# Attention and a feed-forward block on one core: where the second weight matrix, batch 2's transposes and the reserve of feed-forward work stand in the program

## The chip, the cores and the metric

The kernel runs on one core of a Trainium2 chip. A core has a matrix engine (TensorE, PE in the profile), a vector engine (VectorE, DVE), an activation engine (ScalarE, ACT), a general engine (GpSimd, POOL), a queue engine (SyncE, SP) and 16 DMA engines. Each engine runs its own list of instructions in order; they wait for each other by semaphores. The metric is the time of one execution in microseconds of device time, the median of three runs.

## The reference, cut to what matters

```python
# 8 batches, 8 heads, 576 positions, head size 64; 512 model columns, 2048 hidden columns
scores = scale * np.matmul(q, k.transpose(0, 1, 3, 2))
cum    = np.cumsum(np.maximum(s, 0.0), axis=-1)
bias   = -(cum[:, :, :, None] - cum[:, :, None, :])
scores = np.where(causal, -1e9, scores + np.minimum(bias, 0.0))
attn   = softmax(scores)
x      = np.matmul(attn, v)  # then (batch, position, 8 heads * 64)
xn     = (x - mean) / np.sqrt(var + 1e-06) * g_ln
out    = x + np.maximum(xn @ w_ch1, 0.0) @ w_ch2
```

Attention has a bias that sinks with the running sum of a gate, and a causal mask. Its output goes through a layer norm and two matrix products with a ReLU between them.

## The kernel before

**Tiles.** 576 positions are four full tiles of 128 and a tail of 64. q and k of all heads of a batch stand in `aug` as bf16, with four extra columns that carry the running sum (`shift` writes these). Transposed, they stand in `qkT`: 68 rows, 16 heads of q and k. The tails of two batches are put together (`xts`), and those of four batches make one small chunk of the feed-forward block (`tail_chunk`).

**Groups.** The main loop at the end (lines 621 to 642) runs over `g`, one group for each head of each batch: group 8b+h is head h of batch b. A group issues the scores of its head (`score_mms`, line 163), the exponentials on ACT and the mask on POOL (`score_exp`), the products with v of the group before (`values`, line 209), and a number of feed-forward units between them. The values of a batch's last head come at the end of its last group, in `last_of` (line 598).

**Units.** The feed-forward block of a batch (its chunk) is cut into 32 units of four matmuls of 128x512: 16 for the first product and 16 for the second (a tail chunk has 16 units). `chunk_units` appends them to the list `units`; `mlp(n)` takes n from its head and issues them. A chunk can only be appended when its norm has been issued, which is at the end of its batch. So a queue of units of the batch before fills PE beside the attention of the present one. `n_units` (line 620) sets how many each group takes: 2 or 3 in groups 8 to 15, then 4,4,4,4,3,3,3,3 for each batch.

**The end of a batch.** `last_of(b)` issues the last values, then for two halves: statistics and `norm` (DVE writes `xn`, POOL raises the variance to the power -1/2), a DMA transpose of `xn` on SP (`x_t`), and two units.

**How q, k and v come in.** Batches 0 to 2 are loaded head by head into buffers of their own (`homes`), 128 KB a request, all asked for by SP: 24 requests for heads and 3 for tails. Some of these buffers are used again: batch 2's q lies where batch 1's k was, its k where batch 1's v was, its v where batch 1's q was. DVE and POOL cast q and k of a head into `aug` (`cast_head`), PE transposes them (`t_pe`, `t_act`, ten transposes a head), and DVE and ACT copy the two results to `qkT`. From batch 3 on the loads go by tiles through `ring`, ten slots; POOL casts, SP issues DMA transposes (`t_dma`, one for each of the five tiles), and each cast gives a slot back (`room`), which lets `loads()` ask for the next tile.

**What sets the order.** `at(g, pos, f)` hangs a function into group g, at one of the places "a", "a2", "b", "x", "c", "d", "e" in it. On each engine instructions run in the order in which the program issues them; a load waits on SP until its buffer's last reader is through.

Of the kernel before, what the change touches and what calls it, by code (L numbers as in the profile page):

```python
# [16 lines left out]
def kernel(  # L17
# [11 lines left out]
    nc = tc.nc  # L29

    B, H, S, D = q.shape
# [20 lines left out]
    AHEAD = 10  # L52
# [56 lines left out]
    def copy(eng, o, i):  # L109
        if eng == "act":  # L110
            nc.scalar.copy(out=o, in_=i)  # L111
        elif eng == "dve":
            nc.vector.tensor_copy(out=o, in_=i)  # L113
        else:
            nc.gpsimd.tensor_copy(out=o, in_=i)  # L115
# [12 lines left out]
    def shift(b, eng):  # L128
        hb = slice(b * H, (b + 1) * H)
        eng.tensor_scalar_mul(out=aug[:, :, 0:H, D], in0=cumh[:, :, hb, 0], scalar1=-1.0)  # L130
        eng.tensor_copy(out=aug[:, :, H:HD, D1:DK], in_=cumh[:, :, hb, :])
# [6 lines left out]
    def load_w2(i):  # L138
        nc.gpsimd.dma_start(out=w2_bf[:, 4 * i : 4 * i + 4, :], in_=w2_r[:, 4 * i : 4 * i + 4, :])
# [4 lines left out]
    def new_t(b):  # L144
        qkT[b] = tpool.tile([P, HD, SP_], BF16, name="qkT", tag="qkT")

    def t_pe(b, h, engs=("dve", "dve")):
        for j, eng in ((h, engs[0]), (H + h, engs[1])):
            pt = ps_m.tile([P, 2 * 512], BF16, name="pt", tag="pm")
            for p in range(NT):  # L150
                nc.tensor.transpose(pt[0:DK, p * P : (p + 1) * P], aug[:, p, j, 0:DK], ident)  # L151
            copy(eng, qkT[b][0:DK, j, :], pt[0:DK, 0:SP_])

    def t_dma(b, p):
        nc.sync.dma_start_transpose(
            out=qkT[b][:, :, p * P : (p + 1) * P],
            in_=aug[:, p, :, :].rearrange("p h d -> p (h d)"),
        )
# [50 lines left out]
    def values(g):  # L209
        b, h = g // H, g % H  # L210
        pot = pots.pop(g)[0]
        e = ebufs[g % 3]
        for t in range(NT):
            for kb in range(t + 1):
                c = EO[kb] + (t - kb) * P
                if t == NF and b % 2:
                    c -= TL
                nc.tensor.matmul(  # L218
                    pot[:, t * D1 : (t + 1) * D1], lhsT=e[:, c : c + P],
                    rhs=v_bfs[b % 2][:, kb, h, :], start=(kb == 0), stop=(kb == t),  # L220
                )
        xs[b] = xbufs[(2, 1, 0)[b % 3]]
        pv = pot[:, 0 : NT * D1].rearrange("p (t d) -> p t d", d=D1)
        rinv = small.tile([P, NT], F32, name="rinv", tag="rinv")
        rv = rinv.rearrange("p (t o) -> p t o", o=1)
        nc.vector.reciprocal(out=rv, in_=pv[:, :, D:D1])  # L226
        nc.vector.tensor_tensor(  # L227
            out=xs[b][:, :, h * D : (h + 1) * D], in0=pv[:, :, 0:D],
            in1=rv.to_broadcast([P, NT, D]), op=ALU.mult,
        )  # L230
        if h == H - 1:
            lo = TL * (b % 2)
            nc.gpsimd.tensor_copy(
                out=xts[b // 2 % 3][lo : lo + TL, :], in_=xs[b][lo : lo + TL, NF, :]
            )


    units = []
# [15 lines left out]
    def stores(eng, keep=0):  # L254
        while len(late) > keep:
            o, i = late.pop(0)
            eng.dma_start(out=o, in_=i)
# [98 lines left out]
    def mlp(n, eng=None):  # L356
        for _ in range(min(n, len(units))):
            stores(eng or nc.scalar, 0 if eng else 1)
            units.pop(0)()
# [14 lines left out]
    def tails_in(what, b, eng):  # L374
        t = homes[what, b]
        eng.dma_start(
            out=t[0:TL, :, NF, :],
            in_=src[what][b, :, NF * P : S, :].rearrange("h s d -> s h d"),
        )

    def head_in(what, b, h, eng):
        t = homes[what, b]
        eng.dma_start(  # L383
            out=t[:, h, 0:NF, :],
            in_=src[what][b, h, 0 : NF * P, :].rearrange("(t p) d -> p t d", p=P),
        )

    def cast_head(what, b, h, eng):
        i = homes[what, b][:, h, :, :]
        o = v_bfs[b % 2][:, :, h, 0:D] if what == "v" else aug[:, :, (what == "k") * H + h, 0:D]  # L390
        copy(eng, o, i)
# [9 lines left out]
    n_loaded, room = [0], [0]  # L401

    def loads():
        while n_loaded[0] < len(seq) and room[0] > 0:
            key = seq[n_loaded[0]]
            t = ring[:, n_loaded[0] % AHEAD, :]
            room[0] -= 1
            dma_in(t, src_of(src[key[0]], key[1], key[2]), nc.sync)
            staged[key] = t
            n_loaded[0] += 1  # L410

    def casts(what, b, p, eng):
        cast((what, b, p), eng)
        room[0] += 1
# [64 lines left out]
    NG = B * H  # L479
    hooks = {}  # L480

    def at(g, pos, f):
        hooks.setdefault((g, pos), []).append(f)

    def run(g, pos):
        for f in hooks.get((g, pos), ()):
            f()
# [21 lines left out]
    def heads_in(b, hs):  # L509
        for h in hs:  # L510
            for what in "qkv":
                head_in(what, b, h, nc.sync)
# [12 lines left out]
    def tiles(c, i, part, lo, hi):  # L525
        for a in i:
            stats(c, a, part, lo, hi)

    def t_act(b, h):
        t_pe(b, h, ("dve", "act"))  # L530

    def c_head(b, h):
        cast_head("q", b, h, "dve")
        cast_head("k", b, h, "pool")
# [23 lines left out]
    for h in range(H):  # L558
        at(8 + h, "a", lambda h=h: feed(1, h))
        if h >= 2:  # L560
            at(7 + h // 2, "a2" if h % 2 else "c", lambda h=h: t_act(1, h))
    for i in range(4):
        at(9 + i, "e", lambda i=i: load_w2(i))
    for p in (3, 4):
        at(6 + p, "e", lambda p=p: nc.gpsimd.memset(aug[:, p, :, DK:P], 0.0))


    for g, hs in ((9, (0, 1)), (10, (2, 3)), (11, (4, 5))):
        at(g, "b", lambda hs=hs: heads_in(2, hs))

    def b2_rest():
        for what in "qkv":
            tails_in(what, 2, nc.sync)
        heads_in(2, (6, 7))

    at(12, "a", b2_rest)
    at(13, "e", lambda: (new_t(2), shift(2, nc.gpsimd)))
    for h in range(H):
        g = 12 + h // 2
        at(g, "d", lambda h=h: c_head(2, h))  # L580
        at(g + 2, "a2" if h % 2 else "c", lambda h=h: t_act(2, h))
        at(g + 1, "d", lambda h=h: cast_head("v", 2, h, "pool"))

    def more(n):
        room[0] += n

    at(16, "e", lambda: more(AHEAD))


    for b in range(3, B):  # L590
        g0 = 8 * (b - 1) + (2 if b == 3 else 0)
        at(g0, "a", lambda b=b: (shift(b, nc.gpsimd), new_t(b)))
        for p in range(NT):
            at(g0 + p, "d", lambda b=b, p=p: (casts("q", b, p, "pool"), casts("k", b, p, "pool")))
            at(g0 + p + 1, "c", lambda b=b, p=p: t_dma(b, p))
            at(min(g0 + 5 + p // 2, 8 * b - 1), "d", lambda b=b, p=p: casts("v", b, p, "pool"))

    def last_of(b):
        values(8 * b + 7)
        for i in ((0, 1), (2, 3)):  # L600
            tiles(b, i, 1, 256, 512)
            norm(b, i, 2)
            x_t(b, i)
            mlp(2)
        chunk_units(b)

    def tail_chunk(c):
        tiles(c, (0, 1), 0, 0, 512)
        norm(c, (0, 1), 1)
        x_t(c, (0, 1))  # L610
        chunk_units(c)

    for b in range(B):
        at(8 * b + 5, "d", lambda b=b: tiles(b, range(NF), 0, 0, 256))
        if b:
            at(8 * b + 7, "e", lambda b=b: last_of(b))
        if b % 4 == 3:
            at(8 * b + 8, "x", lambda b=b: tail_chunk(B + b // 4))

    n_units = {g: 2 + (g in (9, 11, 13, 14, 15)) if g < 16 else 4 - (g % H > 3) for g in range(H, NG)}  # L620
    for g in range(NG + 4):
        nu = n_units.get(g, 0 if g < H else 4)
        run(g, "a")
        if g >= 3:
            loads()
        if g < NG:
            score_mms(g)
            run(g, "a2")
            score_exp(g, 0)
        mlp(min(1, nu))  # L630
        if g < NG:
            score_exp(g, 1)
        mlp(min(1, nu - 1))
        run(g, "b")
        if 1 <= g <= NG and g % H:
            values(g - 1)
        run(g, "x")
        run(g, "c")
        mlp(min(1, nu - 2))
        run(g, "d")  # L640
        mlp(min(1, nu - 3))
        run(g, "e")
# [32 lines left out]
```

## Time and profile before

| | |
|---|---|
| runs | 394.97, 395.89, 399.01 us |
| the profiled execution | 400.01 us |
| its span, first to last instruction | 398.3 us |
| mean granted clock of TensorE | 0.959 |
| busy in the span | PE 354.4, DVE 201.0, POOL 169.3, ACT 159.4 us |
| moved by DMA | 60.16 MB, mean 151 GB/s |

The page of the profile has a strip of 40 slices of about 10 us for each engine, in which a digit is the busy share in tenths. An answer by windows gives for each stretch its length, then for PE, PEld (weight loads), DVE, ACT and POOL the busy time and the count of instructions, then the granted TensorE clock, the DMA share and GB/s. A timeline row has start, duration, engine, source line, operation, what it writes and reads, its shape and count, and in brackets how long the engine sat idle before it and what ended that wait. Matmuls of PE are pipelined, so a row's duration overlaps the next row's start. Rows of SPq are requests on the DMA queue.

### The profile page before, as it was taken

The page shows a single profiled execution, that of the slowest core. Times are in us where ns is not written, and L with a number is a line of the kernel's source. Part 1 is how long each engine was busy: PE and PEld are TensorE (multiplying, and loading weights), DVE is VectorE, ACT ScalarE, POOL GpSimd, SP SyncE. Part 2 cuts the span into 40 slices and gives each one's busy share as a digit, 9 for nine tenths or more (in the row PEclk, how much of TensorE's full clock was granted, in tenths as well). Part 3 has the DMA queues.
Part 4 walks back from the last instruction along what each step waited for, and adds up shares of the span by engine and source line. Part 5 has one row for each costly group of instructions (what it writes and reads, how often), then busy time and mean ns, then how long its engine had stood idle before and what let it go on. Part 6 is the DMA issues. An engine that isn't in the chain of part 4 may idle for free.

```text
span 398.3 us, 7510 instructions
## 1 busy us (share of the span) xinstructions
PE 354.4 (89%) x2795; PEld 197.4 (50%) x2821; DVE 201.0 (50%) x465; ACT 159.4 (40%) x286; POOL 169.3 (43%) x331
## 2 busy tenths in 40 slices
PE   2865899399999499999997999999999998999995
PEld 1643565265555145554553575545545554444472
DVE  6588453447544614567456234743583259333231
ACT  1463486052664035615641345543553352022020
POOL 5595364446345534357455434554561124100000
PEclk9995799889999879999999899999999999999999
DMA  9999999804999999997999999979612103310112
GB/s 166 220 169 193 225 186 224 155 14 116 225 193 219 178 214 232 205 219 186 186 199 186 203 224 241 195 161 235 133 28 53 55 26 62 98 53 2 70 38 54
DMA packets 191717, 60.16 MB, mean 151 GB/s; under 512 B 182784, under 2 KB 186880, under 8 KB 191680
## 3 DMA queue, kind: packets, MB, share of 16 engines
q1 hardware_dynamic: 181952, 48.00, 65.6%
q0 software_dynamic: 4224, 4.19, 6.8%
q10 hardware_dynamic: 5504, 7.47, 6.3%
q8 instruction: 22, 0.36, 0.4%
q14 instruction: 15, 0.12, 0.1%
HBM read 37.11 MB, written 9.44 MB: 117 GB/s over the span
## 4 chain that ended last, share of the span: by engine, by line
PE 70%; DMA 11%; DVE 7%; SPq 4%; POOL 3%; issue 2%; ACT 2%; ACTq 0%; DVEq 0%; POOLq 0%
PE ph L327 27%; PE py L338 26%; PE s L171 8%; PE pot L218 6%; DMA qkT<-aug 4%; SPq L383 3%; PE pt L151 3%; DVE xn L277 3%; DMA ring<-in_q_dram 2%; DMA ring<-in_k_dram 2%; DVE stats L262 1%; POOL v_bf L115 1%; ACT e L188 1%; DVE hT L312 1%; DMA ring<-in_v_dram 1%
## 5 line engine op out<-in xcount | busy, mean ns | idle before, releaser
L338 PE MATMUL py<-w_bf,hT 128*128 128x512 bf16 x550 | 136.0, 390 | 1.4
L188 ACT ACTIVATE e<-s 128x1024 bf16<-128x1024 f32 (+1 forms) x128 | 97.8, 807 | 93.6 <-PE s L171 73.1
L327 PE MATMUL ph<-xnT,w_bf 128*128 128x512 bf16 x512 | 122.9, 383 | 3.6 <-DVE hT L312 1.9
L191 POOL TENSOR_SCALAR_AFFINE_SELECT e<-e 128x384 bf16<-128x384 bf16 (+1 forms) x128 | 56.5, 465 | 125.4 <-ACT e L188 113.4
L327 PEld LDWEIGHTS <-w_bf 128*128 128x128 bf16 x640 | 59.0, 98 | 54.7 <-issue 6.9
L338 PEld LDWEIGHTS <-hT 128*128 128x128 bf16 x576 | 54.1, 100 | 58.6 <-issue 6.1
L310 ACT ACTIVATE hT<-ph 128x512 bf16<-128x512 f32 x72 | 43.0, 597 | 91.0 <-PE ph L327 88.9
L312 DVE TENSOR_SCALAR hT<-ph 128x512 bf16<-128x512 f32 x72 | 49.4, 690 | 55.6 <-PE ph L327 54.5
L171 PE MATMUL s<-qkT 68*128 68x512 bf16 (+4 forms) x320 | 54.5, 300 | 9.9 <-DMA qkT<-aug 9.1
L171 PEld LDWEIGHTS <-qkT 68*128 68x128 bf16 x384 | 32.9, 99 | 49.4 <-issue 11.4
L344 DVE SCALAR_TENSOR_TENSOR yo<-py,rstd,x 128x512 f32<-128x512 f32 x32 | 24.0, 749 | 60.1 <-PE py L338 57.3
L115 POOL CAST aug<-ring 128x512 bf16<-128x512 f32 (+2 forms) x74 | 39.7, 559 | 17.1 <-DMA ring<-in_k_dram 17.0
L218 PEld LDWEIGHTS <-e 128*128 128x128 bf16 x960 | 38.5, 99 | 13.6 <-issue 0.5
L218 PE MATMUL pot<-v_bf,e 128*128 128x65 bf16 x960 | 40.8, 196 | 0.4 <-POOL e L191 0.4
L226 DVE RECIPROCAL rinv<-pot 128x5 f32<-128x5 f32 x64 | 12.3, 192 | 41.2 <-PE pot L218 37.9
L227 DVE TENSOR_TENSOR x<-pot,rinv 128x320 f32<-128x320 f32 x64 | 31.5, 492 | 2.5 <-DVE rinv L226 0.2
L151 PE MATMUL pt<-ident,aug 128*68 128x128 bf16 x240 | 21.1, 243 | 6.8 <-POOL aug L130 3.1
L111 ACT COPY qkT<-pt 68x640 bf16<-68x640 bf16 x17 | 11.7, 687 | 32.5 <-PE pt L151 27.0
L262 DVE BATCH_NORM_STATS2 stats<-x 128x6 f32<-128x256 f32 (+2 forms) x68 | 23.4, 398 | 0.3
L277 DVE SCALAR_TENSOR_TENSOR xn<-x,mv,gln_b 128x512 bf16<-128x512 f32 x32 | 22.6, 747 | 0.0
L151 PEld LDWEIGHTS <-aug 128*68 128x68 bf16 x240 | 17.8, 130 | 9.3 <-issue 3.2
L113 DVE COPY qkT<-pt 68x640 bf16<-68x640 bf16 x31 | 14.5, 481 | 12.2 <-PE pt L151 12.1
(55 smaller groups left out, 163.9 us busy)
## 6 DMA issues: line engine op xcount, KB each, us to landing
out_dram<-yo ACTq DMA_DIRECT2D x25, 256.0 KB, 3.3
ring<-in_q_dram SPq DMA_DIRECT2D x20, 256.0 KB, 4.3
ring<-in_k_dram SPq DMA_DIRECT2D x20, 256.0 KB, 4.9
ring<-in_v_dram SPq DMA_DIRECT2D x20, 256.0 KB, 4.5
w_bf<-in_moe_w_ch_dram POOLq DMA_DIRECT2D x8, 512.0 KB, 8.6
ring<-in_k_dram SPq DMA_DIRECT2D x31, 128.0 KB, 4.0
ring<-in_q_dram SPq DMA_DIRECT2D x22, 128.0 KB, 4.4
x<-in_v_dram SPq DMA_DIRECT2D x17, 128.0 KB, 4.0
```

Source lines behind the costliest of these rows:

```text
L115: nc.gpsimd.tensor_copy(out=o, in_=i)
L151: nc.tensor.transpose(pt[0:DK, p * P : (p + 1) * P], aug[:, p, j, 0:DK], ident)
L171: nc.tensor.matmul(o, lhsT=qkT[b][0:DK, H + h, kb * P : (kb + 1) * P], rhs=qkT[b][0:DK, h, lo:hi], start=True, stop=True,)
L188: nc.scalar.activation(out=o, in_=i, func=ACT.Exp, scale=scale)
L191: nc.gpsimd.affine_select(out=d, in_=d, compare_op=ALU.is_ge, fill=0.0, base=0, pattern=[[0, d.shape[1]], [1, P]], channel_multiplier=-1,)
L218: nc.tensor.matmul(pot[:, t * D1 : (t + 1) * D1], lhsT=e[:, c : c + P], rhs=v_bfs[b % 2][:, kb, h, :], start=(kb == 0), stop=(kb == t),)
L227: nc.vector.tensor_tensor(out=xs[b][:, :, h * D : (h + 1) * D], in0=pv[:, :, 0:D], in1=rv.to_broadcast([P, NT, D]), op=ALU.mult,)
L277: eng.scalar_tensor_tensor(out=xn[:, j, :], in0=x_of(c, a), scalar=mv[:, j, 0:1], in1=gln_b, op0=ALU.subtract, op1=ALU.mult,)
L310: nc.scalar.activation(out=o, in_=i, func=ACT.Relu)
L312: nc.vector.tensor_scalar_max(out=o, in0=i, scalar1=0.0)
L327: nc.tensor.matmul(ph[:, j * tok : (j + 1) * tok], lhsT=w1_bf[:, kd, fb * P : (fb + 1) * P], rhs=xnT[c][:, :, kd, :], start=(kd == 0), sto ...
L338: nc.tensor.matmul(st["py"], lhsT=st["h"][:, fb, a * P : (a + 1) * P], rhs=w2_bf[:, fb, :], start=(fb == 0), stop=(fb == FB - 1),)
```

## The change

Five things are done.

1. The four loads of the second weight matrix (`load_w2`, on POOL's queue) move from the ends of groups 9 to 12 to the places "b" of groups 8, 8, 9 and 10.
2. Batch 2's loads move from groups 9, 10, 11 and 12 to groups 12, 13 and 14, and its tails go first.
3. Batch 2's casts and transposes, which were spread over groups 12 to 17, go into `second_chunk` at the end of group 15: after `last_of(1)` comes `shift` (on DVE instead of POOL), then for each head one unit, the next head's cast and this head's transposes. The casts of v follow there and in groups 16 and 17.
4. The ten ring slots for batch 3 are released there too, in group 15 instead of 16, and batch 3's casts and DMA transposes begin in group 17 instead of 18.
5. Groups 8 to 15 take two units each. From group 16 on a group takes as many (at most four) as leave ten units queued at the end of its batch.

```diff
-    for i in range(4):
-        at(9 + i, "e", lambda i=i: load_w2(i))
+    for i, g in enumerate((8, 8, 9, 10)):
+        at(g, "b", lambda i=i: load_w2(i))
...
-    for g, hs in ((9, (0, 1)), (10, (2, 3)), (11, (4, 5))):
-        at(g, "b", lambda hs=hs: heads_in(2, hs))
-
-    def b2_rest():
-        for what in "qkv":
-            tails_in(what, 2, nc.sync)
-        heads_in(2, (6, 7))
-
-    at(12, "a", b2_rest)
-    at(13, "e", lambda: (new_t(2), shift(2, nc.gpsimd)))
-    for h in range(H):
-        g = 12 + h // 2
-        at(g, "d", lambda h=h: c_head(2, h))
-        at(g + 2, "a2" if h % 2 else "c", lambda h=h: t_act(2, h))
-        at(g + 1, "d", lambda h=h: cast_head("v", 2, h, "pool"))
-
-    def more(n):
-        room[0] += n
-
-    at(16, "e", lambda: more(AHEAD))
+    def b2_in(g):
+        if g == 12:
+            for what in "qkv":
+                tails_in(what, 2, nc.sync)
+        heads_in(2, range(3 * (g - 12), min(H, 3 * (g - 12) + 3)))
+
+    for g in (12, 13, 14):
+        at(g, "a", lambda g=g: b2_in(g))
+
+    def second_chunk():
+        last_of(1)
+        new_t(2)
+        shift(2, nc.vector)
+        c_head(2, 0)
+        for h in range(H):
+            mlp(1)
+            if h + 1 < H:
+                c_head(2, h + 1)
+            t_act(2, h)
+        for h in range(4):
+            cast_head("v", 2, h, "pool")
+        room[0] += AHEAD
+
+    at(15, "e", second_chunk)
+    for h in range(4, H):
+        at(14 + h // 2, "b", lambda h=h: cast_head("v", 2, h, "pool"))
...
-        g0 = 8 * (b - 1) + (2 if b == 3 else 0)
+        g0 = 8 * (b - 1) + (1 if b == 3 else 0)
...
-        if b:
+        if b > 1:
             at(8 * b + 7, "e", lambda b=b: last_of(b))
...
-    n_units = {g: 2 + (g in (9, 11, 13, 14, 15)) if g < 16 else 4 - (g % H > 3) for g in range(H, NG)}
+    n_units = {g: 2 for g in range(H, 2 * H)}
+    KEEP = 10
     for g in range(NG + 4):
+
         nu = n_units.get(g, 0 if g < H else 4)
+        if 2 * H <= g < NG:
+            nu = max(0, -((KEEP - len(units)) // (H - g % H)))
```

## The prediction

> **What bounds the kernel.** I read the page's slices first, then windows of 10 us, then PE's timeline at the slices where PE sags, then the queues for which PE waited there.
>
> ```profile
> PE   2865899399999499999997999999999998999995
> ...
> 70.00:80.00 10.00, 3.34 (x21) 1.91 (x20) 4.66 (x12) 1.08 (x2) 4.66 (x11) 0.79 0.85 147
> 80.00:90.00 10.00, 9.89 (x104) 6.25 (x105) 5.06 (x14) 4.70 (x9) 4.68 (x12) 0.87 0.07 27
> ...
> 130.00:140.00 10.00, 3.61 (x18) 1.45 (x17) 5.86 (x14) 0.00 (x0) 5.21 (x9) 0.86 1.20 183
> 140.00:150.00 10.00, 9.95 (x56) 4.64 (x57) 2.43 (x5) 3.85 (x7) 4.50 (x10) 0.80 1.18 216
> ...
> 210.00:220.00 10.00, 7.20 (x60) 3.77 (x60) 6.56 (x17) 1.08 (x3) 6.12 (x10) 0.95 1.23 181
> 220.00:230.00 10.00, 9.95 (x73) 6.09 (x73) 2.88 (x5) 3.90 (x9) 4.00 (x8) 0.87 1.31 208
> ```
>
> PE is the bound: 9 in nearly every slice. After the start-up three places sag, at 70, 130 and 210 us. In the windows PE's busy time follows the length; the granted clock and the DMA share come near the end, and the clock is short behind each sag.
>
> ```profile
> 69.92 0.82 PE L171 MATMUL s<-qkT 68*128 68x512 bf16 x5
> 74.32 0.20 PE L171 MATMUL pot<-qkT 68*128 68x64 bf16 x1 [3.58 <-DVE x L227]
> 77.60 1.28 PE L151 MATMUL pt<-ident,aug 128*68 128x128 bf16 x10 [3.08 <-POOL aug L130]
> ...
> 136.50 0.38 PE L171 MATMUL s<-qkT 68*128 68x512 bf16 x1 [3.35 <-DMA qkT<-aug]
> 139.91 1.01 PE L171 MATMUL s<-qkT 68*128 68x64 bf16 x4 [3.04 <-DMA qkT<-aug]
> ...
> 215.57 0.38 PE L171 MATMUL s<-qkT 68*128 68x512 bf16 x1
> 218.71 0.67 PE L171 MATMUL s<-qkT 68*128 68x64 bf16 x4 [2.75 <-DMA qkT<-aug]
> ...
> 72.15 0.88 DVE L113 CAST aug<-ring 128x320 bf16<-128x320 f32 x2 [5.38 <-DMA ring<-in_q_dram]
> ```
>
> Stall A (group 14): batch 2's q comes late, DVE stands 5.38 us in front of its cast, and PE idles 3.58+3.08=6.7 us. Stalls B (group 24) and C (group 40) are waits for the last DMA transposes of batches 3 and 5, 3.35+3.04=6.4 and 2.75 us. The clock missing from the windows (0.21+0.13, 0.14+0.20, 0.05+0.13, times 10 us) makes half-clock stretches of 6.8, 6.8 and 3.6 us; PE worked in about 5, 4 and 3.4 us of them and lost half: 2.5, 2.0 and 1.7 us. So A costs 9.2, B 8.4, C 4.4 us. These 22 us are about all there is to win.
>
> **The change, part by part.** Prices, from undisturbed groups and from batch 1's norm as it runs now:
>
> ```profile
> 121.61 0.82 PE L171 MATMUL s<-qkT 68*128 68x512 bf16 x5
> ...
> 124.02 0.62 PE L218 MATMUL pot<-v_bf,e 128*128 128x65 bf16 x15
> 124.47 1.03 PE L338 MATMUL py<-w_bf,hT 128*128 128x512 bf16 x4
> 125.34 0.82 PE L171 MATMUL s<-qkT 68*128 68x512 bf16 x5
> ...
> 55.74 0.73 PE L151 MATMUL pt<-ident,aug 128*68 128x128 bf16 x10
> 56.30 1.89 PE L327 MATMUL ph<-xnT,w_bf 128*128 128x512 bf16 x8
> ...
> 66.83 0.20 PE L171 MATMUL pot<-qkT 68*128 68x64 bf16 x1 [0.37 <-DVE x L227]
> ...
> 89.04 0.63 PE L218 MATMUL pot<-v_bf,e 128*128 128x65 bf16 x15
> 92.95 0.82 PE L171 MATMUL s<-qkT 68*128 68x512 bf16 x5
> ...
> 94.32 1.40 DVE L277 SCALAR_TENSOR_TENSOR xn<-x,mv,gln_b 128x512 bf16<-128x512 f32 x2
> ...
> 95.22 1.07 POOL L283 TENSOR_TENSOR rstd<-rstd,nhalf 128x2 f32<-128x2 f32 x1
> ...
> L111 ACT COPY qkT<-pt 68x640 bf16<-68x640 bf16 x17 | 11.7, 687 | 32.5 <-PE pt L151 27.0
> L113 DVE COPY qkT<-pt 68x640 bf16<-68x640 bf16 x31 | 14.5, 481 | 12.2 <-PE pt L151 12.1
> ```
>
> From start to start a unit takes 0.87 us, values 0.45, a head's ten transposes 0.56, and a group of three units 3.73, which leaves 0.68 for scores.
>
> *Two units a group in groups 8 to 15* (16 for 21). Group 14's scores move from 69.92 by three units less, 2.6, and by 0.37 more: with two units nothing stands between a group's values and the next scores, which the row at 66.83 shows as a wait, and group 12 now has it too. So 67.7; groups 14 and 15 last 0.68+1.73+0.45+0.37=3.2 up to their values, and values(15) starts at 74.6, with 0.5 us (an estimate) for the mask that it now follows directly.
>
> *Batch 2's transposes behind batch 1's norm.* values(15) at 89.04, last xn done at 95.72, 6.7 us later on DVE, POOL's rstd done at 96.29: this chain stays. Behind it now queue shift (0.4, an estimate: about one cast) and the first casts (0.44, half of the 0.88 at 72.15), so the first transpose is ready some 7.7 us after values(15). PE has values and five units meanwhile, 4.8 us: a **new stall of 2.9 us**. Then come eight heads of 0.56 and seven units, 10.5 us; each head's copies (0.48 on DVE, 0.69 on ACT) and next cast hide behind the unit of 0.87. Uncovered, an ACT copy would cost 0.69 a head, 5.5 us. Group 16 starts at 74.6+7.7+10.5=92.8, against 92.95: no sooner, but with 34 units queued for 37 (2.6 us) and four heads' transposes already done (2.25 us). Of these 5.0 us I take off 0.85, half of C's clock loss, since the clock may or may not fall behind the new stall: **A is worth 4.2 us**.
>
> The Trainium skill, "TensorE: Matmul & The Clock Gate", "What's actually happening", has the clock halved after at least one idle window of about 3.4 us. C differs: 2.75 us of idle time was enough in this trace. By the page's rule the new stall costs no clock and A is worth 5.0; by the row at 218.71 it costs C's whole 1.7 and A is worth 3.3.
>
> *Loads reordered.*
>
> ```profile
> 25.80 2.92 SPq L383 DMA_DIRECT2D ring<-in_v_dram  x1
> ...
> 47.68 0.46 SPq L383 DMA_DIRECT2D ring<-in_q_dram  x1
> ...
> 59.62 2.78 SPq L383 DMA_DIRECT2D ring<-in_k_dram  x1
> ...
> 73.25 0.50 SPq L383 DMA_DIRECT2D x<-in_v_dram  x1
> ...
> 61.09 0.48 POOL L115 CAST v_bf<-ring 128x320 bf16<-128x320 f32 x1
> ```
>
> SP asks for batch 2 from 47.68 already, whatever group the code names: only its order and free buffers count. Now the tails come first, and k's overwrites all of batch 1's v, whose last cast is at 61.09. So the 27 requests start near 61, and the down weights have the DMA alone before. SP's eleven requests from 59.62 to 73.75 took 1.28 us each beside weights; alone one takes 0.5 (73.25). At a mean of 0.9 the last goes out at 85 and lands some 4 us later; head 7 is wanted at 74.6+7.7+7x1.43=92 (1.43 is 0.56+0.87). Cost 0, covered by the norm with 3 us to spare; the third rival prices it uncovered. xnT(1)'s transposes queue on SP behind these 27, but the first unit that reads them comes ten units after last_of(1). The weights are wanted from group 15 on, five groups after the last of their requests; POOL's four issues only change places.
>
> *Batch 3 a group sooner, its loads released at 15 instead of 16.*
>
> ```profile
> 104.96 0.82 PE L171 MATMUL s<-qkT 68*128 68x512 bf16 x5
> ...
> 110.33 4.00 SPq L155 DMA_TRANSPOSE qkT<-aug  x1
> ...
> 132.61 7.26 DMA qkT<-aug
> ...
> 187.33 4.19 SPq L155 DMA_TRANSPOSE qkT<-aug  x1
> ...
> 208.13 10.53 DMA qkT<-aug
> ...
> 178.44 0.82 PE L171 MATMUL s<-qkT 68*128 68x512 bf16 x5
> ...
> DMA to landing us min/median/max: 5.1/6.4/7.0
> ```
>
> The last row is for the five transposes from 145 to 185 us, batch 4's. Batch 3's ten loads wait for batch 2's casts to free their slots, and land before group 17. There the first cast on POOL stands behind the mask and two casts of v that moved (0.9): group 17 starts at 92.8+0.85+3.3=97, and the transpose follows its group's scores by some 6.3 us, 5.4 as in batch 3 now (104.96 to 110.33) and the 0.9: 103.2. From there SP paces, a transpose of about 4 us and two loads at a time: 22.3 us from first to fifth in batch 3, 20.8 in batch 5. Landing took 7.3 and 10.5; the five of batch 4 took 5.1 to 7.0 us. So 103.2+20.8+5=129 to 103.2+22.3+10.5=136; I take 131, nearest to 22.3 and 5 to 7, since fewer of batch 3's own loads are in flight by then. PE is ready at 93.6+8x3.73+3.5=127 (eight groups, last_of(2)'s four units). The stall is 4 us and C's clock loss 1.7: **B is worth 8.4-5.7=2.7 us**. x of values(16) must now wait for the moved v casts; some 0.3 us, left out.
>
> *Ten units kept.* Groups 16 to 23 run three units where they had 4,4,4,4,3,3,3,3 (counted above); 24 to 31 as now; 32 to 63 four each. So batch 4 has four units more, 3.5 us, before group 40. Counted from group 32's scores (178.44), PE was ready for group 40 after 37.1 us and the transpose landed after 40.2; now PE comes after 40.6: **C is worth 4.4 us**. Were the cover gone, all of it would stay. At the end 38 units are left for 53, the same work done sooner, worth nothing by itself.
>
> Sum: 4.2+2.7+4.4=11.3 us off the profiled execution's 400.0, 388.7. The median of the three runs before, 395.89, lies 4.1 under that execution: **384.6 us**.
>
> **The rivals.** *First, B stays:* the five transposes run at 22.3 and the last lands like batch 5's, at 136; PE waits 9 us, B is worth nothing, 387.3. For it speaks the DMA share of 1.2 at 130 us; against it, that the loads of batch 3 are through earlier.
>
> *Second, B goes too:* the last lands at 129, PE waits 2 us, too short for the clock, which doesn't fall behind the norm either. B is worth 6.4, A 5.0, in all 15.8: 380.1. Against it: PE itself comes 6 us sooner.
>
> *Third, slower:* batch 2's requests, held until 61, meet the weights and come late into second_chunk. At r us a request head 7 lands at 61+27r+4. At 1.28 it is 7.6 us late, with 1.7 of clock 9.3, and 2 us of gain are left (394). From r=1.35 on the kernel is slower; at 1.6 it takes 402.5. For it: batch 1's request at 25.80 took 2.92 beside weights. Against: these weights are all asked for before 61 and have the DMA alone till then.
>
> **How the numbers follow.** My forecast 0.45; first rival 0.15; second 0.15; batch 2 late without eating the gain, 387 to 394, 0.15; late past that 0.10. A measurement of this kernel tells about 1% from no change: faster means under 391.9. The first three and half of the fourth give 0.82 faster, the rest of it 0.08 within 1%, the last 0.10 slower. The range takes in the first two rivals and the fourth case, 379 to 393, with some 0.15 outside.
>
> **What would show it.** In the changed profile: A's DVE wait for a load gone; a PE wait of about 3 us for the first transpose of batch 2, behind xn; group 16 near 93 us; a wait of 3 to 6 us for qkT at group 24, near 127; none at group 40. I am wrong if DVE waits for batch 2's loads inside second_chunk, if its heads run slower than 1.43 us, or if group 24's wait is as long as now.

## The result, and the profile after

| | before | after |
|---|---|---|
| runs, us | 394.97, 395.89, 397.37, 399.01 | 384.57, 384.91, 386.22, 386.26 |
| median, us | 396.63 | 385.57 |
| profiled execution, us (span) | 400.01 (398.3) | 386.26 (384.5) |

The changed kernel is faster: the ratio of the times is 0.9715, with a 95% interval of 0.9655 to 0.9774. The time stands 1.0 us from the forecast of 384.6.

First the page's slices and the windows of 10 us of the changed kernel, in the same columns as before.

```profile
PE   2784899979999899999999999999999999989995
...
70.00:80.00 10.00, 9.39 (x84) 5.09 (x87) 6.60 (x19) 3.63 (x7) 3.71 (x7) 1.00 0.88 183
80.00:90.00 10.00, 7.42 (x56) 4.66 (x55) 7.12 (x19) 2.06 (x3) 6.85 (x15) 0.83 0.95 216
...
130.00:140.00 10.00, 8.30 (x50) 4.03 (x51) 3.18 (x8) 3.26 (x6) 4.99 (x10) 0.83 1.19 243
...
210.00:220.00 10.00, 10.00 (x96) 7.70 (x95) 6.01 (x13) 5.64 (x10) 6.62 (x13) 1.00 0.86 175
```

The sag at 70 us has become a smaller one at 80, the one at 130 is down from 6.4 us of idle time to 1.7, and the one at 210 is gone. The clock is short by 0.17 in two windows: behind the start-up two half-clock stretches of 3.4 us (clock 0.50) instead of 6.8, 6.8 and 3.4.

PE's timeline at these places, with DVE and POOL at the first of them. The rows at 94.08 and 95.50 are PE's last two heads of batch 2.

```profile
75.32 1.08 PE L218 MATMUL pot<-v_bf,e 128*128 128x65 bf16 x30
83.29 0.82 PE L151 MATMUL pt<-ident,aug 128*68 128x128 bf16 x10 [2.58 <-DVE aug L113]
...
81.21 1.40 DVE L277 SCALAR_TENSOR_TENSOR xn<-x,mv,gln_b 128x512 bf16<-128x512 f32 x2
82.72 0.90 DVE L113 CAST aug<-ring 128x320 bf16<-128x320 f32 x2
82.12 1.07 POOL L283 TENSOR_TENSOR rstd<-rstd,nhalf 128x2 f32<-128x2 f32 x1
83.14 3.25 POOL L115 CAST aug<-ring 128x320 bf16<-128x320 f32 x8
...
94.08 0.72 PE L151 MATMUL pt<-ident,aug 128*68 128x128 bf16 x10
...
95.50 0.72 PE L151 MATMUL pt<-ident,aug 128*68 128x128 bf16 x10
96.06 0.82 PE L171 MATMUL s<-qkT 68*128 68x512 bf16 x5
...
129.36 0.38 PE L171 MATMUL s<-qkT 68*128 68x512 bf16 x1
131.48 0.60 PE L171 MATMUL s<-qkT 68*128 68x64 bf16 x4 [1.73 <-DMA qkT<-aug]
...
209.92 0.82 PE L171 MATMUL s<-qkT 68*128 68x512 bf16 x5
...
338.11 7.07 PE L327 MATMUL ph<-xnT,w_bf 128*128 128x512 bf16 x32 [2.12 <-DMA xnT<-xn]
```

The new stall is where it was expected: DVE casts the first head right behind xn (82.72 after 81.21), POOL starts its eight k casts right behind rstd, and PE sits idle for 2.58 us. The row at 75.32 is the values of groups 14 and 15, 30 matmuls without a gap. No cast waits for a load: POOL goes through all eight k casts in one piece. At group 24 PE waits 1.73 us for the fifth transpose of batch 3, at group 40 not at all. A wait that did not exist before stands at 338 us, 2.12 us for the last batch's xnT.

Stage by stage, by the first scores of groups 8, 16, 24, 40 and the end (before: 45.48, 92.95, 139.91 after the wait, 218.71 after the wait, 398.3; after: 47.16, 96.06, 131.48, 209.92, 384.5):

| stretch | before | after | work moved into it (+) or out of it (-) | gain |
|---|---|---|---|---|
| to group 8 | 45.5 | 47.2 | 0 | -1.7 |
| 8 to 16 | 47.5 | 48.9 | +2.6 (three units) +2.25 (four heads) | 3.4 |
| 16 to 24 | 47.0 | 35.4 | -3.5 (four units) -2.25 | 5.8 |
| 24 to 40 | 78.8 | 78.4 | +3.5 (four units) | 3.9 |
| 40 to end | 179.6 | 174.6 | -2.6 (three units) | 2.4 |

The sum is 13.8 us, the difference of the two profiled executions; the medians differ by 11.1. The diff touches nothing ahead of group 8; where the 1.7 us of the first stretch come from is said at the end.

### The profile page after: what moved, and what is told of

Its sections match the earlier page's. It is cut to its first block, busy times and chain, and to the rows that moved or that the text cites. A ratio compares the mean times of both kernels' runs of the same rounds, so it can differ in the third digit from the quotient of the medians.

```text
span 384.5 us, 7503 instructions
## 1 busy us (share of the span) xinstructions
PE 352.4 (92%) x2795; PEld 198.2 (52%) x2821; DVE 198.8 (52%) x467; ACT 161.2 (42%) x286; POOL 169.0 (44%) x329
## 4 chain that ended last, share of the span: by engine, by line
PE 79%; DMA 6%; DVE 6%; SPq 4%; issue 2%; ACT 1%; POOL 0%; ACTq 0%; DVEq 0%
PE ph L327 32%; PE py L338 28%; PE s L171 9%; PE pot L218 6%; SPq L383 4%; PE pt L151 3%; DMA ring<-in_q_dram 2%; DMA qkT<-aug 2%; DVE xn L277 1%; DMA xnT<-xn 1%; DMA ring<-in_v_dram 1%; DVE x L227 1%; ACT e L188 1%; DVE yo L344 1%; DVE stats L262 1%
## 5 line engine op out<-in xcount | busy, mean ns | idle before, releaser
L188 ACT ACTIVATE e<-s 128x1024 bf16<-128x1024 f32 (+1 forms) x128 | 99.8, 808 | 99.2 <-PE s L171 98.6
L338 PE MATMUL py<-w_bf,hT 128*128 128x512 bf16 x550 | 132.4, 384 | 1.9 <-DVE yo L344 0.3
L151 PEld LDWEIGHTS <-aug 128*68 128x68 bf16 x240 | 19.0, 133 | 10.3 <-DVE aug L113 3.8
L283 POOL TENSOR_TENSOR rstd<-rstd,nhalf 128x2 f32<-128x2 f32 x18 | 19.4, 1077 | 1.5
```

The lines of the kernel that those rows point to most:

```text
L188: nc.scalar.activation(out=o, in_=i, func=ACT.Exp, scale=scale)
L338: nc.tensor.matmul(st["py"], lhsT=st["h"][:, fb, a * P : (a + 1) * P], rhs=w2_bf[:, fb, :], start=(fb == 0), stop=(fb == FB - 1),)
```

## The experiments

All kernels but the second are edits of the changed kernel. Waits and stretches are those of each one's profiled execution, one for each kernel. The kernel before was run beside each set of kernels and had medians of 395.0 to 397.7 us, so a difference of one or two us between kernels of different sets is not shown by their medians alone.

**Which part brings what.** First the old number of units from group 16 on:

```diff
-    n_units = {g: 2 for g in range(H, 2 * H)}
+    n_units = {g: 2 if g < 16 else 4 - (g % H > 3) for g in range(H, NG)}
...
-        if 2 * H <= g < NG:
-            nu = max(0, -((KEEP - len(units)) // (H - g % H)))
```

> The changed kernel with the old number of units from group 16 on (4,4,4,4,3,3,3,3 a batch). Theory: the reserve of ten units is worth stall C and its clock (4.4 us) and some 2.4 us of small waits behind the norms after group 40, less 2.1 us for the new wait for xnT at 336 us; and with four units more before group 24 the rest of stall B (1.7 us and its clock, about 1.5) goes: about 388 us, with a wait for qkT at group 40 back. Rival: the reserve is worth nothing, 385.6. Second rival: it carries the whole of C and more, and stall B is not touched by it: 390 or over.

It took 391.18 us (390.72 to 392.46; 0.9864 of before, 0.979 to 0.9938), and in another way than I wrote. PE's waits:

```profile
135.68 0.72 PE L171 MATMUL s<-qkT 68*128 68x64 bf16 x4 [3.69 <-DMA qkT<-aug]
140.57 1.67 PE L327 MATMUL ph<-xnT,w_bf 128*128 128x512 bf16 x7 [0.86 <-DMA xnT<-xn]
...
181.10 3.21 PE L327 MATMUL ph<-xnT,w_bf 128*128 128x512 bf16 x8 [3.60 <-DMA xnT<-xn]
```

There is no wait at group 40; there is one for xnT behind groups 24 and 32. With 34 units at group 16 instead of 37, the old pattern leaves two behind last_of instead of five, and the next norm is no longer covered. So a reserve is needed here, but this kernel does not show what became of stall C. Its time lies in the second rival's range, but not for the second rival's reason: counted from group 16's scores PE reached group 24 3.5 us later, as the theory had it, and yet its wait there grew from 1.73 to 3.69 us, since the fifth transpose landed in 9.5 us here (6.8 in the changed kernel).

Then the opposite, the kernel before with only the new rule for units (its last two lines as in the changed kernel):

> The kernel before with only the reserve of ten units from group 16 on. Theory: stalls A and B stay as they are (6.7 and 6.4 us of waiting), C goes: 396.6-4.4-2.4+2.1, about 392. Rival: the reserve alone is worth nothing that can be told, 396.6.

It took 392.98 us (0.9916 of before, 0.9872 to 0.9961), as the theory had it. Stalls A and B stay (4.77+2.95 and 2.35+3.10 us), C is gone, and so are the small waits for hT behind the norms, of which the kernel before has this one and another like it at 298 us; the wait for the last xnT appears (1.77 us).

```profile
260.36 1.89 PE L327 MATMUL ph<-xnT,w_bf 128*128 128x512 bf16 x8 [0.78 <-DVE hT L312]
```

**Batch 3's start.** One number back:

```diff
-        g0 = 8 * (b - 1) + (1 if b == 3 else 0)
+        g0 = 8 * (b - 1) + (2 if b == 3 else 0)
```

> The changed kernel, batch 3's casts and DMA transposes begin in group 18 again instead of 17. Theory: the first cast's place in the groups sets when the five transposes start, and SP's pace does the rest, so the last one lands a group (3.7 us) later: the wait at group 24 grows from 1.7 to about 5.4 us, with more of the slow clock: 389 to 391. Rival: the earlier loads did it, and the place of the casts doesn't matter: 385.6.

389.80 us (0.9849, 0.9751 to 0.9947). The first of the five transposes starts 12.5 us after group 16's scores instead of 9.0, and PE waits 2.20+3.05 us at group 24:

```profile
129.84 0.38 PE L171 MATMUL s<-qkT 68*128 68x512 bf16 x1 [2.20 <-DMA qkT<-aug]
133.26 1.01 PE L171 MATMUL s<-qkT 68*128 68x64 bf16 x4 [3.05 <-DMA qkT<-aug]
```

**The order of loads.** Weights at the ends of groups 9 to 12 and batch 2's heads from group 9 on, as before, with `second_chunk` kept:

```diff
-    for i, g in enumerate((8, 8, 9, 10)):
-        at(g, "b", lambda i=i: load_w2(i))
+    for i in range(4):
+        at(9 + i, "e", lambda i=i: load_w2(i))
...
-    for g in (12, 13, 14):
-        at(g, "a", lambda g=g: b2_in(g))
+    for g, hs in ((9, (0, 1)), (10, (2, 3)), (11, (4, 5))):
+        at(g, "b", lambda hs=hs: heads_in(2, hs))
...
+    at(12, "a", b2_rest)
```

> The changed kernel with the old order of loads: batch 2's heads asked for from group 9 on, its tails late, the down weights at the ends of groups 9 to 12; second_chunk stays. Theory: the order of the loads is covered by batch 1's norm, since the transposes come so much later: no DVE wait for a load in second_chunk and no PE wait for the weights, 385.6 within 1%. Rival: batch 2 or the weights come late without the new order, and DVE or PE waits for them: 388 or over.

385.22 us (0.9699, 0.961 to 0.9787): the same. The order of the loads, the first two things that the change names, is worth nothing that can be measured once the transposes stand behind the norm. PE's wait there is the same, too, but this time the clock stayed at 1.00:

```profile
81.00 0.82 PE L151 MATMUL pt<-ident,aug 128*68 128x128 bf16 x10 [2.57 <-DVE aug L113]
...
80.00:90.00 10.00, 8.38 (x82) 5.68 (x83) 7.09 (x18) 4.03 (x6) 5.68 (x13) 1.00 0.56 132
```

**The new stall.** The first head's casts go ahead of the norm:

```diff
-        last_of(1)
         new_t(2)
         shift(2, nc.vector)
         c_head(2, 0)
+        last_of(1)
```

> The changed kernel with shift and the first head's casts of batch 2 issued ahead of batch 1's norm instead of behind it. Theory: PE's new wait of 2.6 us and the half clock behind it (1.7 us) come from the norm in front of these casts on DVE and POOL alone: both go, 381.3. Rival: what is won there is given back at group 24, since SP's transposes of batch 3 don't move: the wait there grows from 1.7 to about 6 us and the time stays near 385.

382.05 us (0.9738, 0.9562 to 0.9913). The wait is now 1.31 us, at the second head, whose cast still stands behind the norm, and the clock stays at 1.00. At group 24 the wait grew from 1.73 to 2.75 us: one us is given back, not all.

**Stall B's rest.** Batch 3 a group earlier still (`g0 = 8 * (b - 1)`):

> The changed kernel, batch 3's casts and DMA transposes begin in group 16 instead of 17. Theory: as the start of the five transposes follows the place of the first cast, the last lands a group earlier and the wait of 1.7 us at group 24 and its clock (1.5 us) go: 382.4. Rival: batch 3's loads, asked for between 85 and 101 us, are not there yet, the casts wait on POOL, and nothing moves or the mask comes late: 385.6 or more.

385.74 us (0.9847, 0.9691 to 1.0002). My theory fell. The casts were not late and the fifth transpose was issued sooner, but it landed later. These are SP's request, the chain's row for it, the ACT queue's output stores and PE's wait; the same for the changed kernel follow.

```profile
121.98 4.77 SPq L155 DMA_TRANSPOSE qkT<-aug  x1
121.98 10.59 DMA qkT<-aug
122.12 0.34 ACTq L257 DMA_DIRECT2D out_dram<-yo  x1
123.57 0.34 ACTq L257 DMA_DIRECT2D out_dram<-yo  x1
132.61 1.01 PE L171 MATMUL s<-qkT 68*128 68x64 bf16 x4 [3.55 <-DMA qkT<-aug]
```

```profile
105.06 3.39 SPq L155 DMA_TRANSPOSE qkT<-aug  x1
124.61 4.59 SPq L155 DMA_TRANSPOSE qkT<-aug  x1
124.61 6.82 DMA qkT<-aug
122.80 0.34 ACTq L257 DMA_DIRECT2D out_dram<-yo  x1
124.25 0.34 ACTq L257 DMA_DIRECT2D out_dram<-yo  x1
```

Two causes offered themselves for the 10.6 us: more loads behind the transpose on SP (four instead of two), or the two output stores, requested just behind the transpose here and ahead of it in the changed kernel. I took the loads first: all five casts of v of batch 3 into group 23, so that they release no load there.

```diff
-        g0 = 8 * (b - 1) + (1 if b == 3 else 0)
+        g0 = 8 * (b - 1)
...
-            at(min(g0 + 5 + p // 2, 8 * b - 1), "d", lambda b=b, p=p: casts("v", b, p, "pool"))
+            at(23 if b == 3 else min(g0 + 5 + p // 2, 8 * b - 1), "d", lambda b=b, p=p: casts("v", b, p, "pool"))
```

> As e6_b3_earlier (batch 3's casts and transposes from group 16), but batch 3's casts of v all in group 23, so that they release no ring slots, and thus no loads of batch 4, right behind the fifth transpose. In e6 the fifth transpose was issued 26.6 us after group 16's scores, 1.9 earlier than in the changed kernel, but took 10.6 us to land instead of 6.8, with four loads behind it on SP instead of two. Theory: these loads share the DMA with it and stretch its landing; without them it lands in about 7 us, PE's wait at group 24 goes (under 0.5 us) and with it the half clock: 382 to 383, and group 24 to 32 takes some 39 us instead of 43. Rival: the landing is long because the transpose comes so early into a busy DMA: it still takes 10 us, the wait stays at 3.5 us and the time at 385.7.

385.56 us (385.37 to 388.87). With no load behind it the transpose took 8.5 us instead of 10.6 and PE waited 1.79 instead of 3.55, but the time did not move. The loads are a part of it at most.

**Three edits together, then the stores.** First the end of the program alone, fourteen units kept from group 56 on:

```diff
-            nu = max(0, -((KEEP - len(units)) // (H - g % H)))
+            nu = max(0, -(((KEEP if g < 56 else 14) - len(units)) // (H - g % H)))
```

> The changed kernel with fourteen units kept instead of ten at the end of the last batch only (groups 56 to 63). Theory: the wait of 2.1 us for xnT at 336 us is ten units' worth of PE work against the norm and transpose of the last batch; four more cover it: 383.5. Rival: the units are only moved and the same wait comes elsewhere: 385.6.

383.04 us (0.9773, 0.9643 to 0.9903), as expected: the wait for the last xnT is gone, and group 56 to the end takes 91.7 us instead of 94.0. With this, the casts ahead and the early batch 3 in one kernel:

> The three edits together (first casts ahead of the norm, batch 3 from group 16 on, fourteen units kept at the end). Theory: the gains add, 4.3+3.2+2.1: about 376. Rival: they overlap at group 24, where DMA and SP are the limit, and only 4 to 6 us are won: 380 to 382.

381.92 us (0.9744, 0.9609 to 0.9878): the rival. The wait at group 24 was 3.91 us. With the later casts of v and two heads' casts ahead of the norm:

```diff
         c_head(2, 0)
+        c_head(2, 1)
         last_of(1)
         for h in range(H):
             mlp(1)
-            if h + 1 < H:
-                c_head(2, h + 1)
+            if h + 2 < H:
+                c_head(2, h + 2)
             t_act(2, h)
```

> e8_all_three with batch 3's casts of v in group 23 as in e9, and the casts of two heads instead of one ahead of batch 1's norm. Theory: the waits of 3.9 us (group 24) and 1.3 us (second head's cast) and one half clock of 1.7 us go: 381.9-6, about 376. Rival: the norm comes later by the second head's cast and batch 2's transposes or xnT take the wait over; 380 or more.

381.87 us (380.51 to 385.80): the rival again. The fifth transpose went out at 119.04 with nothing behind it on SP for 8 us, and still took 10.09 us to land, so the loads were not the cause. The second expected gain did not come whole either: with two heads cast ahead PE still stood 1.35 us (at 84.0) behind the norm, now for DVE's copy of the first head's q to `qkT`, which comes behind xn on DVE. The rows of that kernel:

```profile
119.04 10.09 DMA qkT<-aug
120.43 0.34 ACTq L257 DMA_DIRECT2D out_dram<-yo  x1
121.88 0.34 ACTq L257 DMA_DIRECT2D out_dram<-yo  x1
129.17 0.60 PE L171 MATMUL s<-qkT 68*128 68x64 bf16 x4 [1.80 <-DMA qkT<-aug]
```

That left the stores. The last kernel is this one with no store kept back in groups 17 to 21, so that the one left over from batch 0 goes out in group 17, and two kept back in groups 22 and 23 until group 24:

```diff
-            stores(eng or nc.scalar, 0 if eng else 1)
+            stores(eng or nc.scalar, 0 if eng else hold[0])
...
+        hold[0] = 0 if 17 <= g < 22 else 2 if 22 <= g < 24 else 1
```

> As e10_best, but the output store that is left over from batch 0 goes out in group 17, and no output store is issued in groups 22 and 23 or in last_of(2). In e10 the fifth transpose of batch 3 was issued 5.6 us sooner than in the changed kernel with no load behind it on SP, and still took 10.1 us to land; while it ran, the ACT queue moved 0.52 MB of output (two stores, from 120.4 and 121.9 us), against 0.39 MB in the changed kernel and 0.02 MB in the kernel before. Theory: the two stores share the 16 DMA engines with it and stretch it; without them it lands in 6 to 7.5 us, before PE gets to group 24, so the wait of 1.8 us and the half clock of 1.7 go: about 378.5. Rival: the DMA is slow for transposes at this place whatever else is queued: it lands in 10 us again, the wait stays and the time at 382.

379.97 us (378.72 to 381.51; 0.9585 of before, 0.9536 to 0.9634), the fastest of all. The transpose went out at 118.99, as in the kernel above, and landed in 6.7 us; group 24 starts without a wait, and the clock stays at 1.00.

```profile
118.99 3.62 SPq L155 DMA_TRANSPOSE qkT<-aug  x1
DMA to landing us min/median/max: 6.7/6.7/6.7
...
127.20 0.95 ACTq L257 DMA_DIRECT2D out_dram<-yo  x2
...
126.42 0.82 PE L171 MATMUL s<-qkT 68*128 68x512 bf16 x5
...
165.24 0.60 PE L171 MATMUL s<-qkT 68*128 68x64 bf16 x4 [1.68 <-DMA qkT<-aug]
```

The theory holds here: the transpose went out at the same time, and without the two stores it landed 3.4 us sooner. Not all of the expected gain came, since a wait of 1.68 us for batch 4's transposes shows up at group 32 (165.24), where there was none. Over the fourteen kernels of this study the pattern is the same: batch 3's fifth transpose took 8.5 to 10.8 us in the five where a store was requested within 3.6 us behind it, and 6.5 to 7.3 in the nine where the stores near it came ahead or none came. Over all 350 DMA transposes of q and k in their profiles it is a tendency, not a rule: the 250 without a store that close behind took 4.4 to 7.8 us (median 5.6), the 83 with one 4.9 to 9.5 (7.6), the 17 with two 6.2 to 10.8 (8.5). So a store can stretch a landing, and every landing longer than 7.8 us had one close behind, but not every store does it. The kernel before is among the nine (7.26); its two stores came right behind the fourth transpose, which took 10.6. So the edit that moved the transposes earlier moved the fifth one in front of the stores.

**Stall C.** Three units instead of four in groups 36 to 39:

```diff
             nu = max(0, -((KEEP - len(units)) // (H - g % H)))
+        if 36 <= g < 40:
+            nu = 3
```

> The changed kernel with three units instead of four in groups 36 to 39, the old pattern, in batch 4 alone. Theory: stall C went because PE comes 3.5 us later to group 40: with the old pattern the wait for batch 5's last transpose is back, 1 to 3 us with or without a half clock of 1.7: 387 to 389. Rival: C was a matter of that one transpose's long landing (10.5 us), which differs from run to run: no wait at group 40, 385.6.

385.29 us (383.70 to 386.79). Between theory and rival, nearer to the rival: counted from group 32's scores PE comes 3.45 us sooner to group 40, and it waits 0.66 us there. (A wait of 1.38 us for hT comes later, at 234.6.)

```profile
203.46 0.38 PE L171 MATMUL s<-qkT 68*128 68x512 bf16 x1
204.51 0.60 PE L171 MATMUL s<-qkT 68*128 68x64 bf16 x4 [0.66 <-DMA qkT<-aug]
```

Batch 5's last transpose landed in 6.5 us here, with one store requested 0.5 us behind it and one ahead. In the kernel before it took 10.53, with two stores 0.6 us behind its request (208.13):

```profile
208.71 0.95 ACTq L257 DMA_DIRECT2D out_dram<-yo  x2
```

## Why the prediction was right, point by point

*Where the time was lost.* Right: the three stalls and their half clocks were nearly all that the change moved (13.8 us less between the profiled executions, of which some 0.7 came from elsewhere), and none of the other engines became the bound.

*The new stall behind the norm.* Right in place and cause: 2.58 us against 2.9, and moving the first cast ahead of the norm (382.05) left 1.31 us of it, at the second head. Eight heads then ran at the pace that was worked out, 1.42 us where the clock was full (94.08 to 95.50). The clock did fall for 3.4 us, so A was worth 3.4 us, not 4.2: of the two values, the one by the trace's own row (3.3). The rule of the Trainium skill, "TensorE: Matmul & The Clock Gate", "What's actually happening", at least one idle window of about 3.4 us, did not hold here as a lower bound of the wait: 2.58 us were enough. But it depends on where the wait falls: 2.57 us in the kernel with the old order of loads and 2.75 in the one with the first cast ahead cost no clock (the last section shows how). The 0.5 us for the mask did not come: PE has no wait in front of the values of group 15. Group 16 came at 96.06, not near 93: 1.7 us of this are the start-up's and 1.7 the clock's.

*The loads.* Right: cost 0. The second of the 27 requests went out at 62.5 us, behind the last cast of batch 1's v, and the last at 82; no cast waited. The old order gave the same time (385.22).

*Batch 3 sooner.* Right in kind, mis-sized: PE waited 1.73 us at group 24, outside the 3 to 6 that I gave as a sign, and B was worth about 6.1 us (5.8, and 0.3 less of slow clock in the next stretch), not 2.7. The first transpose started 9.0 us after group 16's scores, near the 9.6 forecast (103.2 less 93.6). The step that was off is the pace "22.3 us from first to fifth in batch 3, 20.8 in batch 5", from which I took 131 us, nearest to 22.3: it was 19.55, with transposes of 3.2 to 3.5 us on SP before the last instead of 3.2 to 4.3. The landing took 6.8 us, within my 5 to 7 but above the 5.5 that the 131 implies. So, counted from group 16's scores, the last transpose landed after 35.4 us instead of 37.4, and PE was there after 33.7 instead of 33.4. That it landed at 131.4, next to the 131 of the forecast, is luck: group 16 itself came 2.4 us late. That the landing follows the start shows in the kernel one group later (389.80): its first transpose started 3.5 us later, and PE waited 3.5 us longer. What I called SP's and the DMA's pace probably had a part that I did not see: the output stores. The fourth transpose of the kernel before, at 10.6 us, ran beside two of them.

*Ten units kept.* The size was right (C and its clock gone), the reason only half: PE does come 3.5 us later, but with the old three units it would have waited only 0.66 us, since the last transpose no longer met two stores right behind its request. That the two stores caused the 10.5 us of batch 5 was not tried by itself, and one store behind the transpose did no harm in the kernel with three units; it is argued from what the kernel with the held stores showed at group 24 and from the 350 landings. Two things I had not counted: the small waits for hT behind later norms went, as the new rule puts second-product units there, which need no ReLU from DVE, and a wait of 2.1 us for the last xnT came, since ten units (8.7 us) do not cover the last norm and its transpose. Fourteen do.

*The sum.* Forecast 11.3 us: 4.2, 2.7 and 4.4. Measured on the profiled executions 3.4, 6.1 and 5.2, some 0.7 more after group 40, and 1.7 lost before group 8; on the medians 11.1 (the median before is 396.63 with the fourth run, 395.89 when I forecast). That the forecast median is off by only 1.0 us is in part luck: the sum was made for the profiled executions, and there 13.8 us were gained, 2.5 more than forecast, with B and C 4.2 us above their terms and A 0.8 below.

*The rivals.* B did not stay. For B the second rival was nearer than my forecast: it had a wait of 2 us and B worth 6.4, and 1.73 and 6.1 were measured. What it had wrong is the clock, which fell behind both waits, so that A was not worth its 5.0. Batch 2's requests were never late: 26 of them from 62.5 to 82.5 us are 0.77 us each, far from the 1.35 at which the third rival would have decided.

## What to carry to other kernels

When work is moved from one place to another on an in-order engine, write down the full chain in front of it there, and issue what needs nothing of that chain (here two casts) ahead of it. A transfer on the path can be stretched by a store that the program happens to send at the same moment: before moving the transfer, look at what the other queues request in the few microseconds behind it, and hold back what nobody waits for. A reserve of filler work should be sized for each wait that it has to cover, and its kind matters: filler that needs the engine on which the wait hangs stops too (0.78 us behind two norms of the kernel before, where first-product units stood in wait of DVE's ReLU).

## What the runs showed of the hardware that I had not expected

The same idle time on PE may or may not cost a half-clock stretch. Waits of 2.58 us were followed by 3.4 us at half clock in the changed kernel; waits of 2.57 (old order of loads) and 2.75 (first cast ahead) by none; one of 2.75 in the kernel before by 3.4 us. The traces show what decides. The half-clock stretches of a kernel are whole steps of 3.41 us and lie on one grid: in the kernel before they start at 31.36, 75.73, 137.17 and 219.09, which is 13, 18 and 24 steps apart. Below are the steps of this grid around the wait for batch 2's first transpose, two of the changed kernel and then three of the one with the old order of loads.

```profile
81.32:84.73 3.41, 1.44 (x14) 1.02 (x15) 2.78 (x7) 0.58 (x1) 3.26 (x6) 1.00 1.03 225
84.73:88.14 3.41, 3.41 (x21) 2.17 (x19) 1.93 (x4) 0.80 (x2) 3.27 (x9) 0.50 0.99 215
...
76.77:80.18 3.41, 1.66 (x8) 0.57 (x6) 3.41 (x9) 0.00 (x0) 2.19 (x4) 1.00 0.41 80
80.18:83.59 3.41, 2.31 (x25) 1.69 (x26) 2.50 (x8) 1.00 (x2) 3.41 (x8) 1.00 0.52 103
83.59:87.01 3.42, 3.42 (x31) 2.15 (x31) 2.67 (x7) 1.51 (x3) 2.09 (x6) 1.00 0.76 203
```

In the changed kernel PE is idle for 1.97 us of the first step, and the next runs at half clock. In the other the wait lies across the border of two steps, with 1.75 and 1.10 us of idle time in them, and no step is slow. In the fourteen profiles, from 50 to 345 us, all 16 full-clock steps with 1.97 us of idle time or more were followed by a slow one, none with 1.68 or less was, and between 1.73 and 1.88 both happened. So a wait of 2 to 3 us costs a stretch if enough of it falls into one step.

The start-up carries a large part of the difference between the profiled executions. Up to group 8 these kernels do nearly the same work, but its scores start at 44.4 to 47.2 us. The clock's rows from 30 to 50 us go with it: 0.74 in the kernel with the old order of loads (44.4 us), 0.66 in the kernel before (45.5), 0.57 in the changed one (47.2). They are, in this order:

```profile
30.00:50.00 20.00, 14.13 (x139) 9.07 (x140) 14.19 (x42) 9.39 (x17) 9.40 (x19) 0.74 1.20 217
30.00:50.00 20.00, 14.20 (x121) 8.84 (x118) 12.78 (x38) 8.30 (x15) 8.88 (x17) 0.66 1.13 209
30.00:50.00 20.00, 14.75 (x118) 9.70 (x119) 13.29 (x39) 7.12 (x13) 8.99 (x18) 0.57 1.06 194
```

The missing clock times 20 us is 5.2, 6.8 and 8.6 us: stretches of about 10.4, 13.6 and 17.2 us at half clock, in steps of 3.4. All fourteen profiles fall into this order: with three steps group 8 starts at 44.4 to 44.7 us, with four at 45.5 to 46.3, with five at 46.8 to 47.2. This is why the stretch to group 8 shows 1.7 us lost that the change did not lose, and a reason why a difference of one or two us between two medians of these kernels says little by itself.
